# Two matmul groups of an MLP issued as a pair into one PSUM bank

## The chip, the core and the metric

The kernel runs on one core of a Trainium2 chip. TensorE multiplies 128x128 weight tiles with a stream of columns and writes to PSUM; ScalarE (ACT), VectorE (DVE) and GpSimd (POOL) do the rest, SyncE (SP) issues transfers. Each engine takes its instructions in the order in which the program issues them, and engines wait for one another through semaphores. The metric is the device time of one execution in microseconds (us).

## The reference

With x of 2048 tokens by 576 and xn its layer norm, the output is a sum of three parts:

```
xn  = layernorm(x)
qkv = xn @ wqkv                      # 32 heads of 18
a   = softmax over 8 keys, 2 positions apart, of q.k * 18**-0.5;  o = a.v
out = x + o @ wo + relu(xn @ w1) @ w2     # w1: 576 x 4608, w2: 4608 x 576
```

All arrays are float32.

## The kernel before

Tokens are taken in two phases of 1024 (even and odd positions, so that an attention window is a run of neighbours). A phase has 8 tiles of 128 tokens, or 4 token blocks of 256. To keep float32 accuracy, every matrix is split into a high and a low part (`hi` rounded by ACT, `lo` the difference by DVE), and a product is made of hi x hi, lo x hi and hi x lo. With 576 = 4.5 x 128 rows this gives the 14 matmuls of `TERMS`.

The MLP's hidden width is 36 F tiles of 128, in 12 chunks of C = 3. A slot is one (phase, chunk, token block, F tile), 288 in all. It consists of

- `h_mm`, the first product: 14 matmuls of 256 columns into a PSUM tile `ph` (called a ph group below). ACT writes `hhi` = relu of it (L447), DVE writes `hlo`, the rest (L448).
- `o_mm`, the second product: 12 matmuls of 288 columns (a po group) into two tiles `po` of two banks each, summed over the three slots of a token block. After the third, DVE adds both to `X` (L471).

PSUM has eight banks: two for `ph`, four for `po`, two for `pm`, which all other products share. All matmuls of products go through the helper `mm` (L112).

The order is written by hand: a loop over steps n issues, for each n, the weight splits that are due (`run_splits`), the ph group of slot n + 2 (`LAG`), the work listed `at` n, the po group of slot n, the work listed `late` at n, and then background DVE work. So TensorE alternates: one ph group, one po group. The listed work is:

- `make_xt`: transposes of normalized tokens into `xT` (L273, L274 on TensorE, L276 to L279 on ACT and DVE). In the first phase the list `HEAD` places them in the first six steps.
- `qkv_tile`: 14 matmuls of 432 columns into `pm`, at eight successive steps, four times a phase (steps 7, 34, 61, 88 and on).
- `attention`: DVE operations on the keys and values, put into a queue `bg`. `run_bg` takes from it as long as DVE's modelled time is within a margin `M` of TensorE's; the margin depends on n % 3.
- the output projection, steps 123 to 131 of a phase: `wo_a` (late at step n) copies the last columns of a token tile (`od`, L411), transposes it (4 + 1 transposes) and splits the result into `oT`; `wo_b` (at step n + 1) multiplies it with `wo` in 28 matmuls into two `pm` tiles, which DVE adds to `X` (L424).
- near the end of the first phase: loads, statistics, norm and transposes for the second (`z` in the plan).

Weights are loaded into `stp` buffers and split some steps before use; the step is the first entry of a line in `plan`. `w1p` and `w2p` hold four tiles each, `hp` four pairs of `hhi` and `hlo`.

Of the kernel before, what the change touches and what calls it, by code (L numbers as in the profile page):

```python
# [10 lines left out]
F32 = mybir.dt.float32  # L11
F32R = mybir.dt.float32r
# [5 lines left out]
P = 128  # L18
# [3 lines left out]
TBN = 256  # L22
# [3 lines left out]
C = 3  # L26
LAG = 2
# [3 lines left out]
HEADW = (-5, -2, -1, 0, 0, 1)  # L31
# [24 lines left out]
def tile_body(ctx: ExitStack, tc: tile.TileContext, x, wqkv, wo, w1, w2, out):  # L56
# [15 lines left out]
    pool = lambda name, bufs, **k: ctx.enter_context(tc.tile_pool(name=name, bufs=bufs, **k))  # L72
# [7 lines left out]
    w2p = pool("w2p", C + 1)  # L80
    wqp = pool("wqp", 1)
    stp = pool("stp", 4)
    hp = pool("hp", LAG + 2)
    prp = pool("prp", 2)
    lgp = pool("lgp", 2)
    smp = pool("smp", 2)
# [2 lines left out]
    ps_h = pool("ps_h", 2, space=PSUM)  # L89
# [21 lines left out]
    def mm(o, l, r, start, stop, n):  # L111
        nc.tensor.matmul(o, l, r, start=start, stop=stop)  # L112
        t["pe"] += n / 2400.0 + 0.002

    def dve(n):
        t["dve"] += (n + 130) / 960.0
# [16 lines left out]
    def run_splits(n):  # L133
        while staged and staged[0][0] <= n:
            _, split, st = staged.popleft()
            split(st)
            stage_more()
# [14 lines left out]
    W1, W2, WQ, WO = {}, {}, {}, {}  # L152
# [76 lines left out]
    X, XT, XN, MR = {}, {}, {}, {}  # L229
# [62 lines left out]
    TERMS = [(k, k) for k in range(KT)] + [(5 + k, k) for k in range(KT)] + [(4, 4)] + [(k, 5 + k) for k in range(5)]  # L292
# [105 lines left out]
    def run_bg(margin):  # L398
        while bg and t["dve"] + bg[0][0] / 960.0 <= t["pe"] + margin:
            n, f, a = bg.popleft()  # L400
            f(*a)
            dve(n)
# [26 lines left out]
    def done(ph, i):  # L429
        left[ph, i] -= 1  # L430
        if left[ph, i] == 0:
            nc.sync.dma_start(o_v[ph, i], X[ph, i])


    slots = [(ph, c, tb, f) for ph in range(NPH) for c in range(NCH) for tb in range(NTB) for f in range(C)]
    H, PO = {}, {}

    def h_mm(n):
        ph, c, tb, f = slots[n]
        w, xt = W1[ph, c, f], XT[ph, tb]  # L440
        pt = ps_h.tile([P, TBN], F32, name="ph")
        for j, (a, b) in enumerate(TERMS):
            wb = w[:, b // 5, (b % 5) * P : (b % 5 + 1) * P]
            mm(pt, wb, xt[:, a, :], j == 0, j == len(TERMS) - 1, TBN)
        hi = hp.tile([P, TBN], F32R, name="hhi")
        lo = hp.tile([P, TBN], F32R, name="hlo")
        nc.scalar.activation(hi, pt, AF.Relu)  # L447
        nc.vector.scalar_tensor_tensor(lo, pt, 0.0, f32(hi), op0=ALU.max, op1=ALU.subtract)  # L448
        t["dve"] = max(t["dve"], t["pe"] + 0.6)
        dve(TBN)  # L450
        H[n] = (hi, lo)

    def o_mm(n):
        ph, c, tb, f = slots[n]
        hi, lo = H.pop(n)
        w = W2[ph, c, f]
        for k in range(2):
            if f == 0:
                PO[k] = ps_o.tile([P, 2, 512], F32, name="po")
            cs = slice(k * P, (k + 1) * P)  # L460
            for j, (l, b) in enumerate(((hi, 0), (hi, 1), (lo, 0))):
                for h in range(2):
                    mm(
                        PO[k][:, h, 0:D2], l[:, cs], w[:, b, h * D2 : (h + 1) * D2],
                        f == 0 and j == 0, f == C - 1 and j == 2, D2,
                    )
        if f == C - 1:
            for k in range(2):
                i = 2 * tb + k
                acc = X[ph, i].rearrange("p (h c) -> p h c", h=2)  # L470
                nc.vector.tensor_tensor(acc, PO[k][:, :, 0:D2], acc, op=ALU.add)  # L471
                dve(D)
                if c == NCH - 1:
                    done(ph, i)
# [4 lines left out]
    def at(n, f, *a):  # L479
        todo.setdefault(n, []).append((f, a))  # L480
# [3 lines left out]
    def late(n, f, *a):  # L484
        todo_late.setdefault(n, []).append((f, a))

    plan = []
    for ph in range(NPH):
        b = ph * SPP
        for c in range(NCH):  # L490
            for f in range(C):
                s = b + c * SPC + f
                first = ph == c == 0
                plan.append((HEADW[f] if first else s - 5, w1_task, ((ph, c, f), c * C + f)))
                plan.append((HEADW[3 + f] if first else s - 3, w2_task, ((ph, c, f), c * C + f)))
        for u in range(NU):
            s = b + UNIT0 + u * UNIT_STEP
            plan.append((s - 5, wq_tasks, ((ph, u), u)))
            for i in range(NI):
                at(s + i, qkv_tile, ph, u, i)  # L500
            late(s + NI + 1, attention, ph, u)
        s = b + UNIT0 + NU * UNIT_STEP + WO_AT
        plan.append((s - 8, wo_tasks, (ph,)))
        for i in range(NI):
            late(s + i, wo_a, ph, i)
            at(s + i + 1, wo_b, ph, i)
            at(s + i + 1, done, ph, i)
        if ph + 1 < NPH:
            e = b + SPP - SPC
            for i in range(NI):  # L510
                z = e + 3 + 2 * i
                at(z - 6, load_x, ph + 1, i)
                late(z - 2, stats, ph + 1, i)
                late(z - 1, norm, ph + 1, i)
                at(z + 1, make_xt, ph + 1, i)
# [27 lines left out]
    norm(0, 2, True)  # L543
    for z, k, op, *a in HEAD:
        (late if k else at)(z, {"stats": stats, "norm": norm, "xt": make_xt}[op], 0, *a)
    M = (3.0, 1.5, 3.0)
    for n in range(-LAG, len(slots)):
        run_splits(n)
        m = n + LAG
        if m < len(slots):  # L550
            h_mm(m)
        for f, a in todo.pop(n, []):
            f(*a)
        if n >= 0:
            o_mm(n)
        for f, a in todo_late.pop(n, []):
            f(*a)
        run_bg(M[slots[n][3] if n >= 0 else 0])
    assert not todo and not todo_late and not bg and not tasks and not staged
# [26 lines left out]
```

## Time and profile before

| | |
|---|---|
| median of 3 runs | 1194.78 us (1194.58 to 1195.4) |
| profiled execution | 1194.74 us, span 1193.0 us |
| TensorE busy | 1183.8 us (99% of the span) |
| VectorE busy | 812.5 us (68%) |
| ScalarE busy | 310.5 us (26%) |
| granted TensorE clock | 0.998 |
| ph matmuls | 4032, 279 ns each |
| po matmuls | 3456, 293 to 296 ns each |

The span runs from the first to the last instruction. Matmuls are pipelined: one lasts 279 ns from its start to its end, while the next starts some 113 ns after it. So it is the distance between starts that counts, not the length of one. In a timeline row, "x14" means 14 instructions merged, and the length reaches from the first start to the last end. Text in brackets is the idle time ahead of a row and the engine that ended it.

### The profile page before, as it was taken

What the parts mean: (1) busy time and instruction counts of PE and PEld (TensorE: products, weight loads), DVE (VectorE), ACT (ScalarE), POOL (GpSimd) and SP (SyncE); (2) the same over time, 40 slices, a digit from 0 to 9 for tenths busy, and PEclk for the clock granted to TensorE, in tenths of its full rate; (3) what the DMA queues carried; (4) which work ended last, traced back from release to release, by engine and by line L of the source; (5) the groups of instructions that cost most, each with busy time, mean ns of one, the idle gap of its engine ahead of it and who ended that gap; (6) DMA issues with size and microseconds to landing.
All of it is one profiled execution on the core that took longest, in us unless ns stands there. A gap on an engine that the chain in (4) does not pass through costs nothing.

```text
span 1193.0 us, 21739 instructions
## 1 busy us (share of the span) xinstructions
PE 1183.8 (99%) x9016; PEld 1172.8 (98%) x9016; DVE 812.5 (68%) x1269; ACT 310.5 (26%) x790; POOL 40.1 (3%) x63
## 2 busy tenths in 40 slices
PE   8999999999999999999999999999999999999998
PEld 7999999999999999999999999999999999999998
DVE  7516875888687578875573278858767875886732
ACT  5422222131222222322233123122221322222210
POOL 2000000010000000000120000000100000000000
PEclk9999999999999999999999999999999999999999
DMA  5312122130321311402242113031302312212002
GB/s 172 84 32 82 42 76 55 38 107 1 98 58 44 86 33 43 114 11 73 91 130 74 46 54 90 22 85 29 86 21 79 83 38 79 63 42 73 21 1 80
DMA packets 84883, 75.67 MB, mean 63 GB/s; under 512 B 6592, under 2 KB 68288, under 8 KB 84784
## 3 DMA queue, kind: packets, MB, share of 16 engines
q1 hardware_dynamic: 82256, 66.08, 19.7%
q10 hardware_dynamic: 2528, 8.20, 2.4%
q8 instruction: 71, 1.16, 0.4%
q14 instruction: 28, 0.23, 0.1%
HBM read 61.34 MB, written 4.72 MB: 55 GB/s over the span
## 4 chain that ended last, share of the span: by engine, by line
PE 98%; DVE 1%; SPq 0%; ACT 0%; DMA 0%; issue 0%; DVEq 0%; ACTq 0%
PE ph L112 39%; PE po L112 38%; PE pm L112 20%; PE pm L273 1%; PE pm L274 0%; DMA st<-in_w 0%; SPq L235 0%; DVE pr L380 0%; DVE pr L373 0%; SPq L157 0%; SPq L162 0%; SPq L161 0%; PE po L273 0%; ACT xn L257 0%; ACT xn L256 0%
## 5 line engine op out<-in xcount | busy, mean ns | idle before, releaser
L112 PE MATMUL ph<-xT,w1t 128*128 128x256 f32 x4032 | 514.2, 279 | 1.3 <-ACT xT L276 0.6
L112 PEld LDWEIGHTS ph<-xT,w1t 128*128 128x128 f32 x4032 | 491.6, 188 | 2.0 <-ACT xT L276 0.8
L112 PE MATMUL po<-w2t,hhi 128*128 128x288 f32 x2304 | 400.5, 296 | 0.4 <-DVE w2t L143 0.3
L112 PEld LDWEIGHTS po<-w2t,hhi 128*128 128x128 f32 x2304 | 337.0, 188 | 2.0 <-DVE w2t L143 0.5
L447 ACT ACTIVATE hhi<-ph 128x256 fp32r<-128x256 f32 x288 | 110.2, 382 | 531.8 <-PE ph L112 512.5
L112 PE MATMUL po<-w2t,hlo 128*128 128x288 f32 x1152 | 244.7, 293 | 0.0
L448 DVE SCALAR_TENSOR_TENSOR hlo<-ph,hhi 128x256 fp32r<-128x256 f32 x288 | 121.7, 423 | 169.1 <-ACT hhi L447 167.8
L471 DVE TENSOR_TENSOR x<-po,x 128x576 f32<-128x576 f32 x192 | 143.9, 757 | 69.8 <-PE po L112 66.3
L112 PE MATMUL pm<-wq,xT 128*128 128x432 f32 x896 | 185.5, 358 | 0.0
L112 PEld LDWEIGHTS po<-w2t,hlo 128*128 128x128 f32 x1152 | 183.7, 188 | 0.0
L112 PEld LDWEIGHTS pm<-wq,xT 128*128 128x128 f32 x896 | 163.8, 188 | 5.6
L343 DVE TENSOR_TENSOR pr<-qo,k 128x1152 f32<-128x1152 f32 x64 | 85.9, 1349 | 0.0
L373 DVE TENSOR_TENSOR pr<-lg,v 128x1152 f32<-128x1152 f32 x64 | 85.0, 1352 | 0.3
L346 DVE TENSOR_REDUCE lg<-pr 128x64 f32<-128x1152 f32 x64 | 85.0, 1343 | 0.0
L143 DVE TENSOR_TENSOR w2t<-st,w2t 128x576 fp32r<-128x576 f32 x72 | 54.3, 755 | 45.0 <-ACT w2t L146 44.7
L380 DVE TENSOR_TENSOR pr<-pr 128x288 f32<-128x288 f32 (+1 forms) x128 | 70.5, 602 | 0.1
L143 DVE TENSOR_TENSOR w1t<-st,w1t 128x640 fp32r<-128x640 f32 x72 | 59.0, 820 | 15.0 <-ACT w1t L146 14.8
L146 ACT ACTIVATE w2t<-st 128x576 fp32r<-128x576 f32 x72 | 49.1, 684 | 45.0 <-PE po L112 31.0
L146 ACT ACTIVATE w1t<-st 128x640 fp32r<-128x640 f32 x72 | 53.0, 737 | 13.2 <-DMA st<-in_w 13.2
L312 ACT ACTIVATE k<-pm 128x144 f32<-128x144 f32 x64 | 18.7, 292 | 142.8 <-PE pm L112 142.6
L112 PE MATMUL pm<-wq,oT 128*128 128x288 f32 x352 | 51.7, 299 | 0.0
L112 PEld LDWEIGHTS pm<-wq,oT 128*128 128x128 f32 x352 | 47.9, 188 | 1.7
(63 smaller groups left out, 398.0 us busy)
## 6 DMA issues: line engine op xcount, KB each, us to landing
st<-in_w SPq DMA_DIRECT2D x72, 288.0 KB, 3.0
st<-in_w SPq DMA_DIRECT2D x72, 256.0 KB, 3.0
st<-in_wqkv SPq DMA_DIRECT2D x32, 216.0 KB, 3.0
st<-in_w SPq DMA_DIRECT2D x144, 32.0 KB, 2.7
out<-x SPq DMA_DIRECT2D x16, 288.0 KB, 2.1
x<-in_x SPq DMA_DIRECT2D x15, 288.0 KB, 3.9
k<-k ACTq DMA_DIRECT2D x8, 441.0 KB, 3.9
v<-v ACTq DMA_DIRECT2D x8, 441.0 KB, 4.6
```

Source lines behind the costliest of these rows:

```text
L112: nc.tensor.matmul(o, l, r, start=start, stop=stop)
L143: nc.vector.tensor_tensor(lo, src, f32(hi), op=ALU.subtract)
L146: nc.scalar.activation(hi, src, AF.Copy)
L273: nc.tensor.transpose(pa[:, k, :], src[:, k * P : (k + 1) * P], ident)
L312: nc.scalar.activation(k[:, W - 1 + i, :], pq[:, 1, :], AF.Copy)
L343: nc.vector.tensor_tensor(pr[i], q, window(k, i), op=ALU.mult)
L346: nc.vector.tensor_reduce(lg[:, i], pr.pop(i).rearrange(heads, d=Dh), axis=AX.X, op=ALU.add)
L373: nc.vector.tensor_tensor(pr[i].rearrange(heads, d=Dh), e, window(v, i).rearrange(heads, d=Dh), op=ALU.mult)
L380: nc.vector.tensor_tensor(o, z[:, 0:n], z[:, n : 2 * n], op=ALU.add)
L447: nc.scalar.activation(hi, pt, AF.Relu)
L448: nc.vector.scalar_tensor_tensor(lo, pt, 0.0, f32(hi), op0=ALU.max, op1=ALU.subtract)
L471: nc.vector.tensor_tensor(acc, PO[k][:, :, 0:D2], acc, op=ALU.add)
```

## The change

From step 3 on, the ph groups run three slots ahead. At n % 3 == 0 two are issued back to back into the halves of one PSUM bank, and one ACT and one DVE instruction of 512 columns empty the bank; at n % 3 == 1 none is issued; at n % 3 == 2 one is issued, and its emptying comes after `o_mm`. So TensorE's order over three steps becomes ph ph po, po, ph po, with other work of those steps between. The hidden tiles come from two buffers for pairs and one for singles; the margins are 3, 3 and 4 us; w1 is split one step earlier, w2 one step later; the second phase's preparation is one step earlier.

```diff
-    hp = pool("hp", LAG + 2)
+    hp = pool("hp", 2)
...
-    def h_mm(n):
-        ph, c, tb, f = slots[n]
-        w, xt = W1[ph, c, f], XT[ph, tb]
-        pt = ps_h.tile([P, TBN], F32, name="ph")
-        for j, (a, b) in enumerate(TERMS):
-            wb = w[:, b // 5, (b % 5) * P : (b % 5 + 1) * P]
-            mm(pt, wb, xt[:, a, :], j == 0, j == len(TERMS) - 1, TBN)
-        hi = hp.tile([P, TBN], F32R, name="hhi")
-        lo = hp.tile([P, TBN], F32R, name="hlo")
+    def h_mm(*ns):
+
+        z = len(ns)
+        pt = ps_h.tile([P, z, TBN], F32, name="ph")
+        for g, n in enumerate(ns):
+            ph, c, tb, f = slots[n]
+            w, xt = W1[ph, c, f], XT[ph, tb]
+            for j, (a, b) in enumerate(TERMS):
+                wb = w[:, b // 5, (b % 5) * P : (b % 5 + 1) * P]
+                mm(pt[:, g, :], wb, xt[:, a, :], j == 0, j == len(TERMS) - 1, TBN)
+        if z == 2 or ns[0] in (0, 2, 4):
+            hi = hp.tile([P, 2, TBN], F32R, name="hhi2")[:, 0:z]
+            lo = hp.tile([P, 2, TBN], F32R, name="hlo2")[:, 0:z]
+        else:
+            hi = hp.tile([P, 1, TBN], F32R, name="hhi", bufs=1)
+            lo = hp.tile([P, 1, TBN], F32R, name="hlo", bufs=1)
+        return ns, pt, hi, lo
+
+    def h_out(ns, pt, hi, lo):
         nc.scalar.activation(hi, pt, AF.Relu)
         nc.vector.scalar_tensor_tensor(lo, pt, 0.0, f32(hi), op0=ALU.max, op1=ALU.subtract)
         t["dve"] = max(t["dve"], t["pe"] + 0.6)
-        dve(TBN)
-        H[n] = (hi, lo)
+        dve(len(ns) * TBN)
+        for g, n in enumerate(ns):
+            H[n] = (hi[:, g, :], lo[:, g, :])
...
-                plan.append((HEADW[f] if first else s - 5, w1_task, ((ph, c, f), c * C + f)))
-                plan.append((HEADW[3 + f] if first else s - 3, w2_task, ((ph, c, f), c * C + f)))
+                plan.append((HEADW[f] if first else s - 6, w1_task, ((ph, c, f), c * C + f)))
+                plan.append((HEADW[3 + f] if first else s - 2, w2_task, ((ph, c, f), c * C + f)))
...
-                z = e + 3 + 2 * i
+                z = e + 2 + 2 * i
...
-    M = (3.0, 1.5, 3.0)
+    M = (3.0, 3.0, 4.0)
     for n in range(-LAG, len(slots)):
         run_splits(n)
-        m = n + LAG
-        if m < len(slots):
-            h_mm(m)
+        single = None
+        if n <= C:
+            single = h_mm(n + LAG)
+        m = n + C
+        if n >= C and n % C != 1 and m < len(slots):
+            if n % C:
+                single = h_mm(m)
+            else:
+                h_out(*h_mm(m, m + 1))
         for f, a in todo.pop(n, []):
             f(*a)
         if n >= 0:
             o_mm(n)
+        if single:
+            h_out(*single)
         for f, a in todo_late.pop(n, []):
             f(*a)
         run_bg(M[slots[n][3] if n >= 0 else 0])
```

## The prediction

> **What bounds the kernel now.** I read the page's busy times and its chain that ended last first, because they say which engine's lost time is the kernel's lost time.
>
> ```profile
> PE 1183.8 (99%) x9016; PEld 1172.8 (98%) x9016; DVE 812.5 (68%) x1269; ACT 310.5 (26%) x790; POOL 40.1 (3%) x63
> ...
> PE 98%; DVE 1%; SPq 0%; ACT 0%; DMA 0%; issue 0%; DVEq 0%; ACTq 0%
> ```
>
> TensorE has almost no gap, and the chain is TensorE work at 98%. DVE and ACT count only where TensorE waits for them. So the change is priced by two things: what it does to the spacing of matmuls, and which waits of TensorE it uncovers.
>
> Then the timeline of TensorE in an ordinary stretch, for what a switch between first products (ph) and second products (po) costs, and at the kernel's end, where three po groups stand in a row. Columns: start, length, work.
>
> ```profile
> 308.18 0.69 PE L112 MATMUL po<-w2t,hhi 128*128 128x288 f32 x4
> 308.71 0.42 PE L112 MATMUL po<-w2t,hlo 128*128 128x288 f32 x2
> 308.97 0.70 PE L112 MATMUL po<-w2t,hhi 128*128 128x288 f32 x4
> 309.50 0.42 PE L112 MATMUL po<-w2t,hlo 128*128 128x288 f32 x2
> 309.76 1.78 PE L112 MATMUL ph<-xT,w1t 128*128 128x256 f32 x14
> ...
> 1184.03 0.69 PE L112 MATMUL po<-w2t,hhi 128*128 128x288 f32 x4
> ...
> 1185.62 0.70 PE L112 MATMUL po<-w2t,hhi 128*128 128x288 f32 x4
> ...
> 1187.22 0.70 PE L112 MATMUL po<-w2t,hhi 128*128 128x288 f32 x4
> ```
>
> A po group takes 309.76 - 308.18 = 1.58 us (medians over the trace: po 1587 ns, ph 1613 ns). Single starts in that ph group are 119, 116, 118, 122 and 119 ns apart and then 113 to 114: the switch costs ph about 26 ns over 14 x 113.4 = 1587. At 14.34 two ph groups stand in a row, and the second starts at 113 to 114 ns with no slow beginning. A po group behind a po group takes 1187.22 - 1185.62 = 1.60 us, 13 ns more than one behind ph.
>
> Third, the output projection, where each transposed tile is used soon after it is made (the timeline of all engines).
>
> ```profile
> 504.38 0.60 PE L273 MATMUL pm<-ident,qo 128*128 128x128 f32 x4
> 504.81 0.27 PE L274 MATMUL pm<-ident,od 128*128 128x128 f32 x1
> 504.84 1.85 PE L112 MATMUL ph<-xT,w1t 128*128 128x256 f32 x14
> 505.01 0.60 ACT L276 ACTIVATE oT<-pm 128x512 fp32r<-128x512 f32 x1 [1.44 <-PE pm L273]
> 505.64 0.69 DVE L277 TENSOR_TENSOR oT<-pm,oT 128x512 fp32r<-128x512 f32 x1 [1.47 <-ACT oT L276]
> 506.37 0.29 DVE L279 TENSOR_TENSOR oT<-pm,oT 64x128 fp32r<-64x128 f32 x1
> 506.53 3.24 PE L112 MATMUL pm<-wq,oT 128*128 128x288 f32 x22
> ```
>
> Five transposes end, ACT and DVE split them until 506.66, and `wo_b` needs that split and the two PSUM buffers it frees. One ph group lies between and covers just about all of it: only the second `wo_b` matmul is late (third start 0.42 us after the first, against 0.26).
>
> **The change, part by part.**
>
> *Fewer switches.* In the listing of the built program ph follows po 176 times, before 265. Of the 89 gone, some 65 are in plain stretches at 26 ns and 24 beside qkv groups, where the slow start is 17 ns: 1.7 + 0.4 = 2.1 us saved. 62 po groups now stand behind a po group at 13 ns more: 0.8 us lost. Net -1.3. New are 24 switches from po to pm, which the trace lacks; between no cost (ph to pm shows none) and 26 ns they cost 0 to 0.6. Bounds: -2.3 (all 89 at 26, no po loss) to +0.6; I take -1.3, as every row for it is in the trace. The Trainium skill ("TensorE: Matmul & The Clock Gate", Back-to-back issue gap) gives N/2.4 + 2.5 ns from one matmul to the next, with no term for a switch; the trace has 113 where that gives 109 and 131 to 133 where it gives 122.5, and by it this part would be 0.
>
> *The output projection loses its cover.* `wo_a` and `wo_b` keep their steps 123 to 131 of each phase, but at steps n % 3 == 1 no ph group is issued any more; it has moved one step ahead, into the pair. The listing shows transposes directly ahead of `wo_b` for tiles 0, 3 and 6 of both phases, and that the first two `wo_b` matmuls wait for DVE. From the od transpose (504.81) to the third `wo_b` matmul (506.96) the old order takes 2.15 us with 14 ph matmuls inside. The new order takes the same 2.15, since the split ends at the same 506.66, but holds nothing, and those 14 matmuls cost 14 x 113.4 = 1.59 us elsewhere. Six times: +9.5. No queue shortens this: the ACT and DVE lengths are fixed by shape, and both engines are free there (the bracketed idle times). DVE's queue ahead of these splits holds no background work later than the step before.
>
> *Late od copy.* At steps n % 3 == 2 the Relu of the single ph group now stands behind `o_mm` on ACT, since it waits for its one buffer, and the od copy of `wo_a` behind that. Relu takes 0.38 us, od 0.30, started 0.28 apart; ACT answers a matmul 0.30 after its start. So od lands about 0.36 us after TensorE wants it, at steps 125 and 128 of both phases: 4 x 0.36 = +1.4 (bounds 0 and 2.0).
>
> *Better cover where the pair precedes.* Tiles 2 and 5 get 28 ph matmuls ahead of `wo_b`, so the 0.16 us of the second matmul goes: 4 x 0.16 = -0.6. DVE gets margins of 3, 3 and 4 us and runs its background earlier, so the two waits for qo at 534.6 and 1122.9 (0.24 and 0.18) may go: -0.4 (bounds -0.4 and 0).
>
> *The start.* Step 6 issues the pair for slots 9 and 10 right behind the transposes of xt 7, which before stood two steps ahead. By the rows near 39.4 (last transpose 39.42, ACT 39.62 to 40.22, DVE 40.25 to 40.94) the pair starts at 40.28, not 39.45, and halts again at its fifth matmul until 41.0; with about 0.1 us for each restart that is 1.1. At step 3 the pair comes 1.6 us sooner, and hlo of slot 4 now stands behind the two sums into x (1.41 us) on DVE: 0.35. Together +1.4 (bounds 0.8 and 2.0).
>
> *At nothing.* A pair's Relu and difference work on 512 elements in one instruction each, start when the second product is done, and are wanted after po, po, ph, po, some 6.4 us later. If DVE were 5 us late this cover would be gone and po would wait. Sums into x have 3.2 us of ph28 behind them where 1.6 was. w1 splits move one step ahead with their use, w2 splits one step back; both still run over 3 us before their use, and their loads are only reordered on SP. The next phase's x loads, statistics and transposes move one step ahead. On SP the load of x tile 4 waits for the store of tile 0 (2.1 us to landing) that much sooner, with weight loads behind it that are wanted several steps later. POOL's two small operations go with the statistics. Between the last transposes and the pair that uses them stands one po group, as before; were it not enough, 1 us once.
>
> Sum: 9.5 + 1.4 - 0.6 - 0.4 + 1.4 - 1.3 = +10.0. The profiled execution took 1194.74 us (span 1193.0 and 1.7 around it), the median is 1194.78, so no shift: **1204.8**. The bounds together reach from 9.5 + 0 - 0.6 - 0.4 + 0.8 - 2.3 = +7.0 to 9.5 + 2.0 - 0.6 + 2.0 + 0.6 = +13.5, so 1201.7 to 1208.2.
>
> **Rivals.**
>
> *The chains trip the clock.* In the windows view (columns: stretch, busy time of PE, PEld, DVE, ACT, POOL, then the granted clock):
>
> ```profile
> 4.30:7.70 3.40, 1.94 (x16) 1.47 (x14) 2.03 (x6) 0.33 (x1) 1.68 (x4) 1.00 0.95 266
> 7.70:11.10 3.40, 1.71 (x11) 1.27 (x11) 3.10 (x9) 3.34 (x9) 0.75 (x2) 1.00 0.94 263
> 11.10:14.50 3.40, 3.40 (x16) 3.32 (x17) 2.16 (x5) 1.48 (x4) 0.00 (x0) 0.50 0.99 346
> ```
>
> A stretch with TensorE busy 1.71 of 3.40 us was followed by one at half clock; one with 1.94 was not. An uncovered chain leaves it idle some 1.3 us, so busy 2.1: just on the safe side. If it trips, each costs half of 3.4 us, six times 1.7: 1215. Chance 0.08. The Trainium skill (same page, Why this matters for your kernels) allows idle gaps up to about 3 us, by which this rival is out; the trace is less kind, since its stretch was half busy and still lost the clock, so I keep it.
>
> *The uncovered chains do not count,* since something else still holds TensorE there or the wait is not for the split: 1204.8 - 9.5 = 1195.3, no change. Against it is the listing. Chance 0.05.
>
> *Faster: switches are worth more than the rows show.* The place is the end of each of the 96 token blocks, where one ph group was all that covered the two sums into x (1.55 us of DVE); with 28 matmuls there a loss spread thinly might vanish. It decides from 12.4 / 96 = 0.13 us a block beyond what I count; at 0.15 the kernel takes 1204.8 - 14.4 = 1190.4. Against it: the groups table gives po hhi 0.4 us of idle time in the whole run. Chance 0.05.
>
> *The change does not do what it says:* the listing excludes that (94 runs of 28 ph, 62 of 24 po).
>
> **How the numbers follow.** The main case, chains uncovered at full clock, has 0.82. Its bounds hold nearly all of it; I widen them to 1201.0 and 1209.5 for background DVE work that slips ahead of a split once (1.35 us), which leaves out the three rivals. 0.2% is 2.4 us, about what a measurement of this kernel tells from no change: slower 0.90 (main and clock), same 0.05, faster 0.05.
>
> **What would show it.** Right: in the profile after, `wo_b` of tiles 0, 3 and 6 has idle time before it released by DVE oT, near 1.3 us each; ph runs of 28 take 3.20 us; po runs of 24 take 3.19. Wrong: no such idle time, a granted clock below 1 around 500 or 1090 us, or idle time of po released by DVE or ACT in the long middle.

## The result and the profile after

The changed kernel takes 1203.45 us (median of 6 runs, 1203.34 to 1204.84) against 1195.01 for the kernel before: slower by a factor of 1.0074, interval 1.0064 to 1.0084. The profiled execution took 1204.84 us, 10.10 more than the one of before (1194.74); the medians are 8.44 apart. Both traces hold one stretch of 3.41 us at half clock near the start (from 11.08 us before, from 12.55 after), which not every execution has, so below trace is compared with trace.

The page after, in the rows that answer to those shown of before: busy times, chain, and from the groups the product of the output projection.

```profile
PE 1185.7 (99%) x9016; PEld 1172.2 (97%) x9016; DVE 795.8 (66%) x1175; ACT 295.4 (25%) x696; POOL 40.5 (3%) x63
...
PE 97%; DVE 1%; ACT 1%; DMA 0%; issue 0%; POOL 0%; SPq 0%; ACTq 0%; DVEq 0%
...
L112 PE MATMUL pm<-wq,oT 128*128 128x288 f32 x352 | 52.0, 300 | 7.8 <-DVE oT L277 7.8
```

DVE and ACT have 17 and 15 us less to do, and nothing came of it. The number that matters is the last one: TensorE now sits idle for 7.8 us in all in front of the matmuls of `wo_b`, until DVE has split oT. Before, the same row shows no such time:

```profile
L112 PE MATMUL pm<-wq,oT 128*128 128x288 f32 x352 | 51.7, 299 | 0.0
```

The timeline after at the first of the six places (tile 0 of the first phase; rows of weight loads and two rows of ACT are left out):

```profile
509.07 0.60 PE L273 MATMUL pm<-ident,qo 128*128 128x128 f32 x4
509.50 0.27 PE L274 MATMUL pm<-ident,od 128*128 128x128 f32 x1
509.70 0.60 ACT L276 ACTIVATE oT<-pm 128x512 fp32r<-128x512 f32 x1 [1.23 <-PE pm L273]
510.33 0.69 DVE L277 TENSOR_TENSOR oT<-pm,oT 128x512 fp32r<-128x512 f32 x1 [1.33 <-ACT oT L276]
511.06 0.29 DVE L279 TENSOR_TENSOR oT<-pm,oT 64x128 fp32r<-64x128 f32 x1
511.08 0.99 PE L112 MATMUL pm<-wq,oT 128*128 128x288 f32 x4 [1.30 <-DVE oT L277]
```

The chain of ACT and DVE is the one of before, length for length, but no ph group runs beside it. Starts are 1.576, 0.325 and 0.236 us apart from the od transpose to the third `wo_b` matmul: 2.14 us.

An ordinary stretch shows what the change was meant to do:

```profile
313.12 0.69 PE L112 MATMUL po<-w2t,hhi 128*128 128x288 f32 x4
...
314.70 0.70 PE L112 MATMUL po<-w2t,hhi 128*128 128x288 f32 x4
...
316.30 1.78 PE L112 MATMUL ph<-xT,w1t 128*128 128x256 f32 x14
317.92 0.69 PE L112 MATMUL po<-w2t,hhi 128*128 128x288 f32 x4
...
319.50 3.36 PE L112 MATMUL ph<-xT,w1t 128*128 128x256 f32 x28
322.70 0.69 PE L112 MATMUL po<-w2t,hhi 128*128 128x288 f32 x4
```

A token block (three slots) takes 322.70 - 313.12 = 9.58 us: po po (3.18), ph (1.62), po (1.58), ph ph (3.20). Over the trace the medians are 3187, 1613, 1587 and 3200 ns, together 9587; three old pairs of 1587 + 1613 make 9600.

The span cut at the starts of po groups (us, from the two traces):

| stretch | before | after | difference |
|---|---|---|---|
| start to po of slot 0 | 19.13 | 19.61 | +0.48 |
| slot 0 to 12 | 57.58 | 62.29 | +4.71 |
| 12 to 120 | 416.48 | 415.99 | -0.49 |
| 120 to 132 (output projection) | 73.91 | 78.48 | +4.57 |
| 132 to 144 | 41.08 | 41.05 | -0.03 |
| 144 to 264 | 473.28 | 472.36 | -0.92 |
| 264 to 276 (output projection) | 73.77 | 78.38 | +4.61 |
| 276 to the end | 37.73 | 34.88 | -2.85 |

When the po group of slot 12 starts, the new order has already done two more ph groups than the old one, and at slot 276 it has two fewer left. These are 3.2 us that are neither lost nor won. Without them slot 0 to 12 costs +1.5 and the end +0.35. The +0.48 ahead of slot 0 differs from one execution to the next: e1, e4 and e5 below, which have the changed kernel's instructions up to there, take 19.12, 19.27 and 19.18 us. The two projections hold 9.2 of the 10.1 us.

### The profile page after: what moved, and what is told of

It reads as the page before. It is cut to its first block, busy times and chain, and to the rows that moved or that the text cites. A ratio compares the mean times of both kernels' runs of the same rounds, so it can differ in the third digit from the quotient of the medians.

```text
span 1203.0 us, 21330 instructions
## 1 busy us (share of the span) xinstructions
PE 1185.7 (99%) x9016; PEld 1172.2 (97%) x9016; DVE 795.8 (66%) x1175; ACT 295.4 (25%) x696; POOL 40.5 (3%) x63
## 4 chain that ended last, share of the span: by engine, by line
PE 97%; DVE 1%; ACT 1%; DMA 0%; issue 0%; POOL 0%; SPq 0%; ACTq 0%; DVEq 0%
PE ph L112 38%; PE po L112 38%; PE pm L112 20%; PE pm L273 1%; DVE oT L277 0%; ACT oT L276 0%; DMA x<-in_x 0%; PE pm L274 0%; DVE bst L243 0%; DVE x L482 0%; ACT xT L276 0%; DVE w2t L143 0%; ACT xn L256 0%; POOL rstd L248 0%; DVE xn L259 0%
## 5 line engine op out<-in xcount | busy, mean ns | idle before, releaser
L112 PE MATMUL ph<-xT,w1t 128*128 128x256 f32 x4032 | 496.5, 278 | 2.4 <-ACT xT L276 1.2
L112 PEld LDWEIGHTS ph<-xT,w1t 128*128 128x128 f32 x4032 | 481.0, 188 | 3.7 <-ACT xT L276 1.7
L457 ACT ACTIVATE hhi<-ph 128x512 fp32r<-128x512 f32 (+1 forms) x194 | 94.6, 488 | 511.4 <-PE po L112 274.2
L458 DVE SCALAR_TENSOR_TENSOR hlo<-ph,hhi 128x512 fp32r<-128x512 f32 (+1 forms) x194 | 106.5, 549 | 92.9 <-ACT hhi L457 92.6
```

## Experiments

The theory is that the time lies in six uncovered chains of the output projection, with the start and the switches as small terms. The main rivals are a loss spread over the run (two products in one bank, larger ACT and DVE instructions, wider margins) and a clock that gives way.

**e1: cover restored inside the new order.**

```diff
...
+        apart = 123 <= n % SPP <= 131
         if n >= C and n % C != 1 and m < len(slots):
             if n % C:
                 single = h_mm(m)
+            elif apart:
+                hi2 = hp.tile([P, 2, TBN], F32R, name="hhi2")
+                lo2 = hp.tile([P, 2, TBN], F32R, name="hlo2")
+                h_half(m, 0, hi2, lo2)
             else:
                 h_out(*h_mm(m, m + 1))
+        elif n > C and n % C == 1 and apart and m < len(slots):
+            h_half(m, 1, hi2, lo2)
```

`h_half`, left out here, issues one ph group into a bank of its own and empties it by itself into half of the shared hidden tiles.

> Undoes one part of the change: in steps 123 to 131 of each phase the two ph groups of a pair go out one per step again (into the halves of one hidden tile, but from PSUM banks of their own), so a ph group stands between the transposes and wo_b at every step. All else is the changed kernel. Theory of the uncovered chains: the six waits of wo_b at tiles 0, 3 and 6 fall from 1.3 us to none, 6 x 1.59 = 9.5 us come back, and the time is about 1194 us, within 1.5 of the kernel before; the od copies stay late (4 x 0.13 us by the trace of the changed kernel). Rival, that the time is lost all over (two products in one bank, larger ACT and DVE instructions, wider margins): 18 of 288 steps are changed, so at most 1 us comes back and it stays near 1203.

Measured: 1193.56 us (11 runs), ratio to before 0.9994 (0.9985 to 1.0002). The projections take 73.64 and 73.66 us. Changing 18 of 288 steps takes back the projections' whole loss; from the first po group to the end the trace has 1173.81 us against 1173.82 before, since the fewer switches pay for the dearer start and end. The row of `wo_b` in e1's groups:

```profile
L112 PE MATMUL pm<-wq,oT 128*128 128x288 f32 x352 | 51.1, 299 | 0.0
```

**e2: the loss alone, in the kernel before.**

```diff
-        if m < len(slots):
+        early = (124, 127, 130)
+        if m < len(slots) and n % SPP not in early:
             h_mm(m)
+        if (n + 1) % SPP in early:
+            h_mm(m + 1)
```

> The loss alone, in the kernel before: only the ph groups of steps 124, 127 and 130 of each phase are issued one step earlier, right behind the ph group of that step. No pairs in a bank, no merged ACT or DVE instructions, old margins. Theory of the uncovered chains: six chains lie bare, +9.5 us, less 4 x 0.16 for the tiles that get two ph groups as cover and less two waits for qo if they move: 1203.5 to 1204.5. Rival (loss from pairs or evacuation): 1195.

Measured: 1202.83 us, ratio 1.0072 (1.0058 to 1.0086). Six ph groups moved one step, with no pair in a bank and no merged evacuation, make the loss. The total is 0.7 us under the expected span; by stretches the projections take 78.11 and 78.05, +4.20 and +4.28, and their sum 8.48 is 9.5 less 0.64 (better cover where two ph groups stand) and less 0.42 (the waits for qo), as in the prediction's sum. Its row shows the same wait:

```profile
L112 PE MATMUL pm<-wq,oT 128*128 128x288 f32 x352 | 52.1, 301 | 7.8 <-DVE oT L277 7.8
```

Two other waits of TensorE grew in e2: po starts 0.29 us late at 258.26, where the trace of before has no wait, and 0.63 late at 851.15, where it has 0.20. In both places DVE came late to the sums that free `po`. Up to 258 us TensorE, ACT and DVE run the same instructions in the same order in both kernels, so a wait of that size comes and goes without any edit.

**e3: pairs emptied in two halves.**

```diff
-        nc.scalar.activation(hi, pt, AF.Relu)
-        nc.vector.scalar_tensor_tensor(lo, pt, 0.0, f32(hi), op0=ALU.max, op1=ALU.subtract)
+        for g in range(len(ns)):
+            q = slice(g, g + 1)
+            nc.scalar.activation(hi[:, q], pt[:, q], AF.Relu)
+            nc.vector.scalar_tensor_tensor(lo[:, q], pt[:, q], 0.0, f32(hi[:, q]), op0=ALU.max, op1=ALU.subtract)
```

> The changed kernel with the order of TensorE kept, but each pair emptied by two ACT and two DVE instructions of 256 columns instead of one of 512 each: DVE gets about 94 x 0.15 = 14 us more work, ACT about 94 x 0.17 = 16. Theory that emptying is off the path (some 6 us of slack): no change, 1203 to 1205, with the same six waits. Rival, that ACT and DVE time sets part of the end: slower by up to 10 us or more.

Measured: 1204.51 us (4 runs), ratio 1.0086 (1.0070 to 1.0101), not to be told from the changed kernel's 1.0074. DVE is back at 807.5 us, ACT at 308.4, and from the first po group to the end the trace has 1183.95 us against 1183.43. So emptying is off the path, and the merged instructions neither gain nor lose more than that.

**e4: another cover.**

```diff
-            at(s + i + 1, wo_b, ph, i)
-            at(s + i + 1, done, ph, i)
+            put = late if (s + i + 1) % C == 1 else at
+            put(s + i + 1, wo_b, ph, i)
+            put(s + i + 1, done, ph, i)
```

> The changed kernel with another cover: at the steps without a ph group wo_b is issued behind the po group instead of ahead of it, so the po group (1.59 us) hides the chain. Theory of the uncovered chains: 9.5 us come back, but now the transposes of the next tile stand right behind wo_b and wait for DVE to add its two pm tiles (two of 0.41 us, begun some 0.2 after the last matmul), about 0.65 us six times: 1203.5 - 9.5 + 3.9 = 1198. Rival (loss not in these chains): 1203 to 1207.

Measured: 1197.45 us, ratio 1.0028 (1.0018 to 1.0039), 6.0 below the changed kernel where 5.6 was expected. The old wait is gone and the expected new one stands there; from e4's waits (columns: total us, times, longest) and timeline:

```profile
PE pm L273 <- DVE x L424: 2.5, 6, 0.4
```

```profile
514.80 0.82 DVE L424 TENSOR_TENSOR x<-pm,x 128x288 f32<-128x288 f32 x2 [1.75 <-PE pm L112]
515.31 0.66 PE L273 MATMUL pm<-ident,qo 128*128 128x128 f32 x4 [0.42 <-DVE x L424]
```

The next tile's transposes wait for DVE to free `pm`; at 515.31 the start is 0.71 us behind the one ahead of it where 0.13 is usual, 0.58 more, and there are six such places. So it is the cover that counts, not which work gives it; a po group does it too, at the price of the next chain.

**e5: the start undone.**

```diff
...
-        if n <= C:
+        if n <= 9:
             single = h_mm(n + LAG)
...
-        if n >= C and n % C != 1 and m < len(slots):
+        if n >= 9 and n % C != 1 and m < len(slots):
```

> The changed kernel with the start undone: single ph groups two slots ahead up to step 9, pairs from there on, so that the pairs at steps 3 and 6 no longer stand right behind the transposes of xt 5 and xt 7. By the trace of the changed kernel the waits there are worth 0.5 us near 31 and 1.0 near 42: theory of the start, 1203.5 - 1.5 = 1202. Rival (the waits at the start are hidden by something later): 1203.5.

Measured: 1203.41 us (1202.43 to 1204.73): by the total, a miss, for no gain shows. By stretches it came and went. Slot 0 to 12 takes 60.73 against 62.29 us (-1.56, as expected). But 144 to 264 takes 0.80 more than in the changed kernel: po waited there for the sums into x twice, at 744.77 and 843.58, with DVE held up by weight splits, the first time by one of w1 whose transfer was late. And the last stores ended 1.0 us later after the start of the last matmul (5.24 against 4.27). That these two are chance and not the edit wasn't tried by itself; waits of that kind come without an edit in e2, and e6 has the same start and neither.

**e6: everything covered.** e1 and e5 together, with the od copy issued ahead of the po group and the last single ph group held back one step (the parts of e1 and e5 are left out):

```diff
+            at(s + i, wo_od, ph, i)
             late(s + i, wo_a, ph, i)
...
             if n % C:
-                single = h_mm(m)
+                if m < len(slots) - 1:
+                    single = h_mm(m)
...
+        if n == len(slots) - C:
+            single = h_mm(n + LAG)
```

> The version that the runs point to: one ph group per step in steps 123 to 131, pairs from step 9, the od copy issued ahead of the po group, and the last single ph group held back one step so that the last token block does not put po behind po. What is left of the change is the fewer switches. Theory: before less 1.3, 1193.2; with the bounds of the switches 1192.2 to 1194.5.

> e6 once more, on the chip of e8, since the half-clock stretch near the start came in some runs of the kernel before and in none of e6's: a second trace for the time from the first po group to the end (1171.7 in the first), and whether its total stays near 1191.6 or is up to 1.5 us longer where that stretch comes.

Measured: 1191.58 us, ratio 0.9969 (0.9958 to 0.9981), and on another chip, as e9, 1192.57, ratio 0.9981 (0.9973 to 0.9990). So this version beats both kernels. e6 came out below the 1192.2 that was the least expected, and e9 lies inside that range. All of e6's runs had a granted clock of 1.000; e9's lay between 0.998 and 1.000 and ran from 1191.03 to 1193.34, longer with the lower clock. From the first po group to the end, which leaves the start's clock out, the traces have 1171.72 and 1171.83 us against 1173.82 before: 2.0 to 2.1 us less.

**e7 and e8: the same without pairs.** e6 with one ph group at every step; e8 has the old margins as well:

```diff
-        apart = 123 <= n % SPP <= 131
+        apart = True
...
-    M = (3.0, 3.0, 4.0)
+    M = (3.0, 1.5, 3.0)     # e8 alone
```

> The kernel of e6 with one ph group per step everywhere, each emptied by itself: the same lead, buffers, margins and split steps, but the old alternation. Against e6 it tells what the fewer switches are worth by themselves. Theory: 86 fewer switches into ph at 17 to 26 ns less 60 po groups at 13 ns more, e7 is 1.3 us slower than e6, about 1194.5. Rival 1 (switches are worth nothing): equal to e6. Rival 2 (pairs save much more, by fewer evacuations): e7 slower by 3 us or more.

> e7 with the margins of the kernel before (3, 1.5 and 3 us). In e7 po waited for the sums into x (five times, up to 1.1 us) because DVE was let run further ahead than one ph group covers; the margin of 1.5 keeps it back. Theory: those waits go, and what is left against e6 is the switches alone: from the first po group to the end 1.2 to 1.5 us longer than e6 (1171.7 by its trace), so about 1173.1. Rival 1, that the switches are worth nothing: 1171.7. Rival 2, that e7 lost its time otherwise than by the margins: over 1178.

e7 measured 1202.2 us, ratio 1.0055 (1.0043 to 1.0068), far above what any reading of the switches allows. Its waits and its timeline (rows of TensorE and DVE) say why:

```profile
PE po L112 <- DVE x L497: 3.1, 5, 1.1
```

```profile
248.19 1.78 PE L112 MATMUL ph<-xT,w1t 128*128 128x256 f32 x14
...
248.90 0.81 DVE L143 TENSOR_TENSOR w1t<-st,w1t 128x640 fp32r<-128x640 f32 x1
249.63 0.60 DVE L143 TENSOR_TENSOR wq<-st,wq 128x432 fp32r<-128x432 f32 x1
250.15 1.41 DVE L497 TENSOR_TENSOR x<-po,x 128x576 f32<-128x576 f32 x2
251.04 0.77 PE L112 MATMUL po<-w2t,hhi 128*128 128x288 f32 x4 [1.08 <-DVE x L497]
```

DVE, let run 3 us ahead, comes late to the sums that free `po`, and a single ph group (1.6 us) does not cover that; two do. These five waits are 3.1 us; its view of waits has three more of TensorE that e6 lacks, for a w2 split (1.1), hlo (0.9) and hhi (0.4). So e7 told of the margins and not of the switches. e8 differs from e7 in the margins alone and measured 1195.04 us, ratio 1.0007 (0.9997 to 1.0016). From the first po group on its trace has 1174.40 us, 6.9 less than e7's 1181.27: the margins were most of e7's loss, and rival 2 of e8 is out. It is still 2.6 to 2.7 more than e6 and e9, where 1.2 to 1.5 was expected. Of that, 0.9 are two late starts of ph, at 93.99 and 310.93, which e6 lacks; 1.7 to 1.8 are left for switches and small waits together. Rival 1 (nothing) is out too.

## Why the prediction was right

- *Sum.* +10.0 was forecast against the profiled execution and +10.10 measured there; the median moved by 8.4. That the traces agree to 0.1 us is luck. From the first po group on the difference is 9.6, and the 0.48 ahead of it is chance; within the 9.6 the od term is 0.9 too large, and 0.35 at the end was put at nothing. Why the median moved by less is not shown. The trace is of the longest of the six executions; four of them lie at 1203.3 to 1203.6, and e3, whose trace has no half-clock stretch, reaches slot 0 in 17.61 us instead of 19.61, so a different share of executions with that stretch is likely.
- *Uncovered chains, +9.5.* Right in place, number, release and length (2.15 forecast, 2.14 measured). The two projections together, with the od copies and the better cover, show 9.2. e1 takes the loss away, e2 makes it alone.
- *Late od copy, +1.4.* Right in kind, too large: the od transpose starts 0.24 us behind the one ahead of it where 0.11 is usual, 0.13 four times, so 0.5. In the trace of the changed kernel the Relu starts at 524.22, while `o_mm`'s last two matmuls, which read hlo, are still running. It waits for the last reader of hhi, not for the end of `o_mm`; those two matmuls, 0.26 us, are about what the step overlooked.
- *Better cover and qo, -1.0.* e2's stretches fit the sum of both terms to 0.1 us, and the two waits for qo, 0.24 and 0.18 us in the trace of before, are gone from the one after.
- *The start, +1.4.* Measured +1.5. The forecast put the pair of slots 9 and 10 at 40.28 for a wanted 39.45, a wait of 0.83; it is 42.79 for a wanted 41.97, 0.82.
- *The switches, -1.3.* In the three stretches without start, projection and end the change saves 1.44 us. Of it 0.28 is a late po at 845.75, where the sums into x came late behind a w2 split; whether it went by the better cover or by chance is not shown. Without it 1.2 is left; e6 against e8 gives up to 1.8. The upper bound of +0.6 left out the 0.8 that po behind po loses, which did no harm. The Trainium skill ("TensorE: Matmul & The Clock Gate", Back-to-back issue gap), whose formula is for an isolated matmul and has no term for a switch, differs from these runs. Switches are worth something, though little.
- *At nothing.* Wrong once: the last token block has no ph group ahead of its first po group, since all had been issued, and po waits 0.31 us for the sums at 1194.03. The term "3.2 us behind them" held for the other 95 blocks. e6 repairs it.
- *Clock rival.* The forecast 2.1 us busy of 3.4 is what the windows view of the changed kernel shows, and the granted clock (1.00, third number from the end) held:

```profile
508.00:511.40 3.40, 2.10 (x16) 1.73 (x14) 1.69 (x4) 1.44 (x5) 0.00 (x0) 1.00 0.00 0
509.50:512.90 3.40, 2.10 (x15) 1.72 (x14) 2.50 (x4) 0.96 (x3) 0.00 (x0) 1.00 0.00 0
```

But the busy share does not carry the argument. Near its start the same trace lost the clock behind a stretch busy for 2.03 of 3.41 us (first two rows, of the changed kernel), and e6 kept it behind one busy for 1.91 (last two):

```profile
9.14:12.55 3.41, 2.03 (x12) 1.62 (x13) 3.29 (x7) 2.80 (x6) 0.75 (x2) 1.00 0.91 297
12.55:15.96 3.41, 3.41 (x18) 3.41 (x17) 2.92 (x9) 1.77 (x4) 0.75 (x2) 0.50 0.98 358
...
4.97:8.38 3.41, 1.91 (x15) 1.45 (x14) 2.47 (x7) 1.07 (x4) 1.06 (x3) 1.00 0.84 243
8.38:11.79 3.41, 2.11 (x14) 1.55 (x13) 3.22 (x9) 3.32 (x8) 0.75 (x2) 1.00 0.97 299
```

So "just on the safe side" at 2.1, taken from one trace, was nearer to the edge than it looked, and that the clock held was in part luck. What the traces do keep apart is the count of matmuls (in brackets behind TensorE's busy time): 11 to 13 in the stretch ahead of each of the six drops, 14 or more in the others looked at, 15 and 16 at the chains. That the count decides was not tried.

- *Other rivals.* The chains count, and the ends of token blocks held no hidden loss: e6, with all covered, gains 2.1 us in 96 blocks, 0.02 each, not 0.13. The split into 94 runs of 28 ph matmuls and 62 of 24 po is what the trace has.

## What to carry to other kernels

When work is taken out of a step to be merged elsewhere, ask first what it stood in front of: here a group of matmuls between a transpose and its use was worth its full 1.6 us as cover, some sixty times a saved switch (26 ns). Merge where nothing leans on the cover, and keep one group per step where a short chain over other engines must end. Margins of background work belong to the cover they were set for; changing one without the other cost 7 us in e7 (against e8).

## Of the hardware

- In the traces of before and after, po matmuls behind ph start 130 to 133 ns apart for the first eight, and then every fourth distance is 140, also across the join of two po groups (medians). ph matmuls behind po start slower for five (118, 117, 117, 122, 118 ns), then keep 113. A switch costs its successor 17 to 26 ns, and po behind ph is 13 ns shorter than po behind po (1587 against 1600).
- A switch from po to pm, which the trace of before lacks, costs nothing to speak of: in the changed kernel the pm group takes 2740 ns behind po against 2737 behind ph.
- The granted clock fell to half near the start in six of the eleven traces, once in each, for 3.41 us, behind a stretch in which TensorE was busy for 1.69 to 2.03 of 3.41 us. A stretch busy for 1.85 (e4, from 4.45 us) passed without a drop, and so did the uncovered chains, at 2.05 to 2.11.
